# Softmax sums moved from GpSimd to VectorE, reciprocals to ScalarE as logarithm and exponential, with more buffers and a new order of steps

## Chip, cores and metric

The kernel runs on one core of one Trainium2 chip. The metric is the device time of one execution in microseconds (us). The kernel before takes 196.88 us, the median of 3 runs (196.62 to 197.10).

## What is computed

A layernorm `xn` of 2048 tokens of 512 features feeds two branches, which are summed with the input:

```python
# A: linear attention with a softmax feature map, 32 heads of 16
pq = einsum("bhsd,hdf->bhsf", q, w_phi); pk = einsum("bhsd,hdf->bhsf", k, w_phi)
phi_q = concat([softmax(pq), softmax(-pq)], -1)      # 16 + 16 features a head
phi_k = concat([softmax(pk), softmax(-pk)], -1)
kv = einsum("bhsf,bhsd->bhfd", phi_k, v);  z = phi_k.sum(over s)
o = (phi_q @ kv) / (phi_q @ z + 1e-6)                # then @ wo
# B: h = xn @ w1 + b1; act = h * tanh(softplus(h)); act @ w2, with 1792 hidden features
out = x + A(xn) + B(xn)
```

## The kernel before

Tokens are in 16 tiles of 128 and in four groups of four tiles. A short head loads the inputs, folds `w_phi` into the key weights and normalises the first group. All the rest is the list `STEPS`, a table of step names that one loop at the end of the kernel executes in the order in which it is written. Each step records its instructions; every engine executes its own in that order, and waits on semaphores for the others. So the table sets the order on each engine, and a step that waits holds back all that stands behind it on its engine.

The letters, with a group, stage or tile number behind them:

- `LN g`, `AP g k`: layernorm statistics of a group and their use on two tiles (VectorE, a little on GpSimd), then a transposing DMA into `xnT`.
- `V t`, `L s i`: one projection of four matmuls to values, or to logits; `VC`, `LC` evacuate them, on ScalarE (`a`) or VectorE (`v`). Stages `s` 0 to 3 are the keys of the four groups, 4 to 7 the queries. `F`, `FC` fold the query weights, from a transposed load `WT`.
- `H u`, `M u`: one of 56 hidden blocks, four matmuls (TensorE), and its Mish (ScalarE).
- `E s 0`, `E s 1`: maximum and minimum of each 16 logits by a tree of four VectorE operations, then a subtraction, into the tile `e`. `X s k`: the exponential of half a stage (ScalarE, in place).
- `S s k`: the sums of each 16 exponentials. In 15 of 16 cases they run on GpSimd (`p`), as a tree of four additions in `sums`; `S 6 0` runs on VectorE, one reduction.
- `R s k`: keys only, the inverses of the sums: a VectorE reciprocal, then a copy that doubles it, on VectorE (`v`) or GpSimd (`p`). `N s k`: the exponentials times the inverses (VectorE). `A g k`: 16 small matmuls a tile that accumulate keys times values. `KV`: the accumulated block masked into `kvm`.
- `W s k`: queries; the ratio of two sums, then one half of the features times it (VectorE), and two transposing DMAs into `qT`. `Q h i`: eight small matmuls against `kvm`; `G h i`: two ScalarE copies, numerators to `nm` and denominators to `ds`. `C h` (`combine`): reciprocal, doubled copy, product (VectorE), and a transposing DMA into `oT`.
- `O t`, `P t`, `Y t`: second layer (14 matmuls), output projection (4) and the residual with the store.

PSUM has six rotating banks for the projections, hidden blocks and outputs (tag `mm`) and one two-bank slot for `pkv`, `pnd` and `pwide`. The transposing DMAs and nearly all stores go through SP's queue.

Of the kernel before, what the change touches and what calls it, by code (L numbers as in the profile page):

```python
# [20 lines left out]


STEPS = """
LN 1; V 0; V 2; H 0; VC 2 a; H 1; M 0; M 1; H 2; H 3; H 4; M 2; H 5; H 6; M 3; M 4; M 5; E 0 0; E 0
1; M 6; H 7; H 8; M 7; H 9; H 10; M 8; M 9; AP 1 0; H 11; H 12; H 13; M 10; M 11; M 12; M 13; AP 1
1; LN 2; LN 3; V 1; L 1 0; VC 0 v; WL 1; X 0 0; V 3; L 1 3; VC 1 a; H 14; AP 2 0; AP 2 1; X 0 1; AP
3 0; S 0 0 p; LC 1 0 v; LC 1 3 a; V 5; VC 3 a; LC 1 1 v; H 15; M 14; AP 3 1; WL 2; M 15; VC 5 a; LC
1 2 v; E 1 0; H 16; H 17; V 4; M 16; M 17; H 18; M 18; H 19; M 19; H 20; H 21; M 20; M 21; VC 4 v; S
0 1 p; H 22; H 23; M 22; M 23; E 1 1; R 0 0 p; V 7; VC 7 v; X 1 0; V 6; L 2 0; LD; L 2 3; WT; R 0 1
v; L 2 2; S 1 0 p; LC 2 0 v; LC 2 3 a; L 2 1; LC 2 2 a; X 1 1; F 0; FC 0 a; S 1 1 p; H 24; M 24; VC  # L30
6 v; H 25; N 0 0; H 26; H 27; N 0 1; A 0 0; H 28; A 0 1; H 29; M 25; M 26; M 27; H 30; M 28; LC 2 1
v; E 2 0; F 1; H 31; M 29; V 11; R 1 0 p; M 30; E 2 1; M 31; H 32; M 32; L 3 0; F 2; X 2 1; S 2 1 p;
LC 3 0 a; L 3 2; L 3 1; FC 1 v; LC 3 2 v; V 8; X 2 0; S 2 0 p; VC 8 a; VC 11 v; LC 3 1 v; N 1 0; L 3
3; H 33; H 34; H 35; M 33; M 34; R 1 1 v; A 1 0; FC 2 v; H 36; LC 3 3 v; V 13; N 1 1; M 35; H 37; M
36; F 3; A 1 1; E 3 0; H 38; FC 3 a; H 39; H 40; M 37; M 38; L 4 1; L 4 0; M 39; E 3 1; V 9; VC 13
a; VC 9 v; M 40; LC 4 0 v; X 3 0; S 3 0 p; V 15; VC 15 v; V 12; L 4 2; LC 4 2 a; L 4 3; LC 4 3 a; H
41; X 3 1; V 10; R 2 1 v; VC 10 a; H 42; H 43; R 2 0 v; N 2 0; M 41; VC 12 a; S 3 1 p; A 2 0; N 2 1;
M 42; H 44; M 43; A 2 1; LC 4 1 v; H 45; M 44; E 4 0; E 4 1; M 45; R 3 0 p; H 46; H 47; H 48; M 46;
O 0; M 47; M 48; X 4 0; S 4 0 p; L 5 0; LC 5 0 a; R 3 1 v; N 3 0; L 6 2; N 3 1; V 14; L 5 2; L 5 1;
VC 14 a; LC 5 2 a; LC 5 1 a; X 4 1; L 5 3; LC 5 3 v; L 6 1; A 3 0; A 3 1; E 5 0; S 4 1 p; H 49; H  # L40
50; M 49; M 50; H 51; M 51; H 52; H 53; H 54; M 52; W 4 0; E 5 1; M 53; M 54; L 6 0; O 1; KV; X 5 0;
Q 0 0; G 0 0; L 6 3; LC 6 0 a; LC 6 1 v; H 55; W 4 1; LC 6 2 v; Q 0 1; G 0 1; C 0; O 2; O 3; LC 6 3
a; Q 1 0; M 55; O 4; X 5 1; G 1 0; E 6 0; S 5 0 p; W 5 0; E 6 1; Q 1 1; G 1 1; L 7 0; P 0; C 1; LC 7
0 a; P 1; X 6 0; O 5; Y 0; Y 1; S 5 1 p; Q 2 0; G 2 0; L 7 1; L 7 2; Q 2 1; W 5 1; P 2; P 3; LC 7 2
a; G 2 1; LC 7 1 a; S 6 0 v; W 6 0; L 7 3; C 2; Y 2; Q 3 0; O 6; LC 7 3 a; G 3 0; Q 3 1; O 7; O 8; P
4; Y 3; E 7 0; X 6 1; E 7 1; G 3 1; Q 4 0; O 9; P 5; Y 4; O 10; X 7 0; X 7 1; G 4 0; Q 4 1; G 4 1; C
3; P 6; P 7; S 6 1 p; W 6 1; Q 5 0; S 7 0 p; Y 5; W 7 0; O 11; G 5 0; Y 6; Y 7; Q 5 1; O 12; G 5 1;
Q 6 0; O 13; C 4; C 5; G 6 0; Q 6 1; P 8; P 9; S 7 1 p; G 6 1; W 7 1; Q 7 0; P 10; Y 8; Y 9; Y 10; C
6; P 11; G 7 0; Q 7 1; G 7 1; O 14; O 15; P 12; P 13; C 7; P 14; Y 11; Y 12; Y 13; Y 14; P 15; Y 15
"""  # L50


# [1 line left out]
def kernel(  # L54
# [164 lines left out]

    def mish(u):
        g, f = divmod(u, FT)
        nc.scalar.activation(  # L224
            acts[:, f, g * 512 : (g + 1) * 512], ph_of.pop(u)[:], ACT.Mish, bias=b1f[:, f : f + 1]
        )
# [6 lines left out]

    def take(s, i, copy):
        if i == 0:
            p_of[s] = smx.tile([P, TPG, 512], BF16, name="p_sb", bufs=1)
        copy(p_of[s][:, i, :], pl_of.pop((s, i)))  # L237

    def extremes(s, pl):

# [4 lines left out]
        src = pv
# [40 lines left out]
    def sums(s, k, pooled=False):

        t = smx.tile([P, 128], FP32, name="s")
        s_of[s, k] = t
        src = pair(s, k).rearrange("p t j l (c e) -> p (t j l c) e", e=16)  # L290
        if not pooled:
            nc.vector.reduce_sum(t[:], src, axis=AX.X)
            return
        for half in (8, 4, 2, 1):
            h = smx.tile([P, 128, half], FP32, name=f"h{half}", bufs=1)[:] if half > 1 else t[:, :, None]
            nc.gpsimd.tensor_tensor(  # L296
                out=h, in0=src[:, :, 0:half], in1=src[:, :, half : 2 * half], op=ALU.add
            )
            src = h

    r_of = {}

    def invert(s, k, pooled):

        t = s_of.pop((s, k))
# [8 lines left out]
    def normalise(s, k):

# [3 lines left out]
            op=ALU.mult,  # L319
        )  # L320

    def weigh(s, k):
# [4 lines left out]
        nc.vector.reciprocal(r[:], t[:, :, 1, :])
        nc.vector.tensor_tensor(  # L328
            out=r2[:], in0=t[:, :, 0, :, None].to_broadcast([P, 16, 4, 2]),
            in1=r[:, :, :, None].to_broadcast([P, 16, 4, 2]), op=ALU.mult,  # L330
        )
# [76 lines left out]
    def combine(h, parts=(slice(0, 2),)):

        nm, ds = nd_of.pop(h) if parts[-1].stop == 2 else nd_of[h]  # L410
        if h not in oT_of:
            oT_of[h] = lnp.tile([P, 8, P], BF16, name="oT")
        for q in parts:
            n = q.stop - q.start
            w = opool.tile([P, 2, 32], FP32, name="w")
            f = opool.tile([P, 2, 32, 2], BF16, name="f")
            nc.vector.reciprocal(w[:, q], ds[:, q].rearrange("p i j c -> p i (j c)"))
# [4 lines left out]
            v = nm[:, q].rearrange("p i j (c e o) -> p (i j c) e o", e=8, o=2)
            nc.vector.tensor_tensor(
                out=v, in0=v,
                in1=f[:, q].rearrange("p i c o -> p (i c) o")[:, :, None, :].to_broadcast(
                    [P, n * 32, 8, 2]
                ),
                op=ALU.mult,
            )
            nc.sync.dma_start_transpose(  # L430
                out=oT_of[h][:, 4 * q.start : 4 * q.stop, :],
                in_=nm[:, q].rearrange("p i j c -> p (i j c)"),
            )
# [164 lines left out]
```

## Time and profile before

| | |
|---|---|
| median of 3 runs | 196.88 us |
| the profiled execution's own time, and its span | 196.23 us, 194.5 us |
| mean granted TensorE clock | 0.982 |
| 40 to 50 us: busy PE, DVE, ACT, POOL | 8.14, 9.79, 8.39, 3.57 of 10 |
| 80 to 90 us | 6.35, 9.72, 7.70, 4.29 |
| 110 to 120 us | 7.08, 9.65, 4.24, 6.06 |
| 130 to 140 us | 7.38, 9.66, 3.59, 5.07 |
| 150 to 160 us | 9.95, 9.67, 2.38, 5.06 |
| 170 to 180 us | 9.89, 5.69, 2.24, 0.17 |
| granted clock, 50 to 60 and 120 to 130 us | 0.83, 0.85 |

PE is TensorE, DVE VectorE, ACT ScalarE, POOL GpSimd. A stretch's busy time counts an engine's own instructions; what it lacks to 10 us is waiting. The granted clock is the share of TensorE's full speed (2.4 GHz) that the chip gave.

### The profile page before, as it was taken

What the parts mean: (1) busy time and instruction counts of PE and PEld (TensorE: products, weight loads), DVE (VectorE), ACT (ScalarE), POOL (GpSimd) and SP (SyncE); (2) the same over time, 40 slices, a digit from 0 to 9 for tenths busy, and PEclk for the clock granted to TensorE, in tenths of its full rate; (3) what the DMA queues carried; (4) which work ended last, traced back from release to release, by engine and by line L of the source; (5) the groups of instructions that cost most, each with busy time, mean ns of one, the idle gap of its engine ahead of it and who ended that gap; (6) DMA issues with size and microseconds to landing.
All of it is one profiled execution on the core that took longest, in us unless ns stands there. A gap on an engine that the chain in (4) does not pass through costs nothing.

```text
span 194.5 us, 2775 instructions
## 1 busy us (share of the span) xinstructions
PE 173.2 (89%) x1023; PEld 83.9 (43%) x1039; DVE 167.5 (86%) x247; ACT 113.2 (58%) x153; POOL 88.1 (45%) x85
## 2 busy tenths in 40 slices
...
GB/s 149 310 401 172 109 17 191 310 277 19 0 0 0 0 3 0 0 0 0 5 0 0 0 3 108 110 54 19 102 175 164 82 27 57 135 192 185 110 110 108
DMA packets 44361, 18.02 MB, mean 93 GB/s; under 512 B 36796, under 2 KB 43836, under 8 KB 44348
## 3 DMA queue, kind: packets, MB, share of 16 engines
...
## 4 chain that ended last, share of the span: by engine, by line
DVE 56%; PE 31%; ACT 6%; issue 4%; DMA 2%; POOL 0%; DVEq 0%; POOLq 0%; ACTq 0%
DVE m L248 18%; DVE e L257 10%; PE ph L214 8%; PE po L442 8%; PE pproj L192 6%; DVE m L254 4%; PE po L450 3%; DVE e L335 3%; ACT e L272 3%; PE warm L496 3%; DVE q L328 3%; DVE p_sb L237 2%; DVE r L309 2%; DVE x_sb L458 2%; DVE e L317 2%
## 5 line engine op out<-in xcount | busy, mean ns | idle before, releaser
L214 PE MATMUL ph<-xnT,w_sb 128*128 128x512 bf16 x224 | 53.6, 390 | 3.2 <-DVE p_sb L237 2.3
L296 POOL TENSOR_TENSOR h<-e 128x1024 f32<-128x1024 bf16 x15 | 33.4, 2226 | 45.5 <-ACT e L272 31.5
L442 PE MATMUL po<-w_sb,acts 128*128 128x512 bf16 (+1 forms) x233 | 50.1, 366 | 2.8 <-ACT p_sb L237 2.6
L224 ACT ACTIVATE acts<-ph,b1f 128x512 bf16<-128x512 f32 x56 | 37.0, 691 | 8.7 <-PE ph L214 8.5
L296 POOL TENSOR_TENSOR h<-h 128x512 f32<-128x512 f32 (+1 forms) x30 | 34.4, 1147 | 2.4
L272 ACT ACTIVATE e<-e 128x2048 bf16<-128x2048 bf16 x16 | 30.5, 1914 | 8.4 <-DVE e L257 8.3
L214 PEld LDWEIGHTS <-w_sb 128*128 128x128 bf16 x224 | 22.0, 100 | 30.0 <-issue 7.0
L442 PEld LDWEIGHTS <-acts 128*128 128x128 bf16 x238 | 22.7, 98 | 25.9 <-issue 2.8
L192 PEld LDWEIGHTS <-xnT 128*128 128x128 bf16 x192 | 18.6, 99 | 25.9 <-issue 4.7
L248 DVE TENSOR_TENSOR m<-m 128x512 bf16<-128x512 bf16 (+1 forms) x32 | 22.0, 689 | 1.1
L192 PE MATMUL pproj<-wqk,xnT 128*128 128x512 bf16 x62 | 16.4, 395 | 3.1 <-ACT p_sb L237 1.9
L272 ACT ACT_TABLE_LOAD x7 | 9.0, 1283 | 16.5 <-DVE e L257 16.4
L458 DVE TENSOR_TENSOR x_sb<-po,x_sb 128x512 bf16<-128x512 f32 (+1 forms) x17 | 10.7, 653 | 8.5 <-PE po L450 8.5
L248 DVE TENSOR_TENSOR m<-p_sb 128x1024 bf16<-128x1024 bf16 x16 | 16.2, 1012 | 0.4
L192 PE MATMUL pproj<-wv,xnT 128*128 128x512 bf16 x59 | 15.5, 379 | 0.3
L237 ACT CAST p_sb<-pproj 128x512 bf16<-128x512 f32 x19 | 10.8, 587 | 8.1 <-PE pproj L192 4.3
L450 PE MATMUL po<-wqk,oT 128*128 128x512 bf16 (+1 forms) x65 | 14.7, 366 | 0.2
L401 ACT COPY ds<-pnd 128x32 f32<-128x32 f32 x16 | 2.9, 184 | 18.8 <-PE pnd L387 18.8
L192 PE MATMUL pproj<-wkp,xnT 128*128 128x512 bf16 x55 | 13.2, 379 | 0.2 <-DVE xnT L179 0.2
L257 DVE TENSOR_TENSOR e<-p_sb,m 128x2048 bf16<-128x2048 bf16 x8 | 12.4, 1544 | 0.6
L317 DVE TENSOR_TENSOR e<-e,r 128x2048 bf16<-128x2048 bf16 x8 | 11.3, 1438 | 0.1
L296 POOL TENSOR_TENSOR s<-h 128x128 f32<-128x128 f32 x15 | 10.8, 717 | 1.2
...
## 6 DMA issues: line engine op xcount, KB each, us to landing
...
```

Of the source, the lines that this page charges most:

```text
L192: nc.tensor.matmul(pp, lhsT=xnT[:, t, kt, :], rhs=w[:, kt, :], start=(kt == 0), stop=(kt == KT - 1),)
L214: nc.tensor.matmul(ph_of[u][:], lhsT=w1_sb[:, kt, f * P : (f + 1) * P], rhs=xnT[:, g * TPG : (g + 1) * TPG, kt, :], start=(kt == 0), stop= ...
L224: nc.scalar.activation(acts[:, f, g * 512 : (g + 1) * 512], ph_of.pop(u)[:], ACT.Mish, bias=b1f[:, f : f + 1])
L237: copy(p_of[s][:, i, :], pl_of.pop((s, i)))
L248: nc.vector.tensor_tensor(out=m[:], in0=src[:, :, 0:half], in1=src[:, :, half : 2 * half], op=op)
L257: nc.vector.tensor_tensor(out=e_of[s][:].rearrange("p t j l c -> p (t j) l c")[:, :, pl, :].rearrange("p t (c e o) -> p t c e o", e=8, o=2 ...
L272: nc.scalar.activation(v, v, ACT.Exp)
L296: nc.gpsimd.tensor_tensor(out=h, in0=src[:, :, 0:half], in1=src[:, :, half : 2 * half], op=ALU.add)
L317: nc.vector.tensor_tensor(out=vv, in0=vv, in1=r_of.pop((s, k))[:, :, None, :].to_broadcast([P, 128, 8, 2]), op=ALU.mult,)
L442: nc.tensor.matmul(po[:, c], lhsT=acts[:, f, t * P : (t + 1) * P], rhs=w2_sb[:, f, c], start=(f == 0), stop=False,)
L450: nc.tensor.matmul(po[:, c], lhsT=oT_of[t // 2][:, t % 2 * 4 + j, :], rhs=wo_sb[:, j, c], start=False, stop=(j == 3),)
L458: nc.vector.tensor_tensor(out=y, in0=po[:, c], in1=y, op=ALU.add)
```

## The change

`STEPS` is rewritten, and five functions change. Every `S` runs on VectorE. All eight `R` and all eight `C` take their inverse on ScalarE as exp(-log(s)), and one of eight `W` (`W 5 1`) its ratio as exp(log a - log b). One table set holds logarithm and exponential, and is asked for ahead of the step. The logits tile `p_sb` has two buffers for one, `e` three for two, `ds` four for two; the numerators `nm` and the transposed `oT` now lie in memory of weights and of `xnT` that is no longer read. Evacuations by VectorE: 7 of logits for 13, 5 of values for 7, 1 of folded weights for 2; the others go to ScalarE. Of the table, two rows, from the middle:

```diff
-E 0 0; ... S 0 0 p; ... R 0 0 p; ... W 4 0; E 5 1; M 53; M 54; L 6 0; O 1; KV; X 5 0; Q 0 0; G 0 0
+E 0 0; ... S 0 0; ... R 0 0 a; ... W 4 0 v; S 4 1; L 7 3; LC 7 3 a; L 7 2; LC 7 2 a; H 52; KV; Q 0 0; G 0 0
```

```diff
+    tables = [None]
+    def table(name):
+        if tables[0] != name:
+            tables[0] = name
+            if name != "mish_and_others":
+                nc.scalar.preload_act_table_set(name)
...
-            p_of[s] = smx.tile([P, TPG, 512], BF16, name="p_sb", bufs=1)
+            p_of[s] = smx.tile([P, TPG, 512], BF16, name="p_sb")
...
-            e_of[s] = epool.tile([P, TPG, 8, 2, 64], BF16, name="e")
+            e_of[s] = epool.tile([P, TPG, 8, 2, 64], BF16, name="e", bufs=3)
...
+    def sums(s, k):
+        t = s_of[s, k] = smx.tile([P, 128], FP32, name="s")
+        nc.vector.reduce_sum(
+            t[:], pair(s, k).rearrange("p t j l (c e) -> p (t j l c) e", e=16), axis=AX.X
+        )
+    def power(out, src, n, scale):
+        table("natural_log_exp_and_others")
+        nc.scalar.activation(
+            out, src.rearrange("p (c o) -> p c o", o=1).to_broadcast([P, n, 2]), ACT.Exp, scale=scale
+        )
+    def log(src, n):
+        table("natural_log_exp_and_others")
+        t = smx.tile([P, 128], FP32, name="log")
+        nc.scalar.activation(t[:, 0:n], src, ACT.Ln)
+        return t[:, 0:n]
+    def invert(s, k, how):
+        t = s_of.pop((s, k))
+        r2 = r_of[s, k] = smx.tile([P, 128, 2], BF16, name="r2")
+        if how == "a":
+            power(r2[:], log(t[:], 128), 128, -1.0)
             return
...
+        if how == "a":
+            t4 = log(t[:], 128).rearrange("p (t l c) -> p t l c", l=2, c=4)
+            nc.vector.tensor_tensor(
+                out=q[:], in0=t4[:, :, 0, :], in1=t4[:, :, 1, :], op=ALU.subtract
+            )
+            power(r2[:].rearrange("p t c o -> p (t c) o"), q[:].rearrange("p t c -> p (t c)"), 64, 1.0)
...
+            half = (wkp, wv)[h // 2 % 2][:, 2 * (h % 2) : 2 * (h % 2) + 2, :]
...
+    def combine(h, how):
+        nm, ds = nd_of.pop(h)
+        oT_of[h] = xnT[:, 2 * h : 2 * h + 2, :, :].rearrange("p t k c -> p (t k) c")
+        f = opool.tile([P, 64, 2], BF16, name="f")
+        d = ds[:].rearrange("p i j c -> p (i j c)")
+        if how == "a":
+            power(f[:], log(d, 64), 64, -1.0)
```

The first place is VectorE at the keys of groups 2 and 3 (`s` sums, `r2` doubled inverses, `e` exponentials). Before:

```order
L309 RECIPROCAL r_990<-s_766 128x128
L310 COPY r2_991<-r_990 128x256
L309 RECIPROCAL r_1005<-s_794 128x128
L310 COPY r2_1006<-r_1005 128x256
L317 TENSOR_TENSOR e_708<-e_708,r2_1006 128x2048
```

Now, at the keys of groups 1 and 2:

```order
L301 TENSOR_REDUCE s_790<-e_547 128x128
L336 TENSOR_TENSOR e_484<-e_484,r2_758 128x2048
L301 TENSOR_REDUCE s_877<-e_484 128x128
L301 TENSOR_REDUCE s_884<-e_547 128x128
L336 TENSOR_TENSOR e_484<-e_484,r2_879 128x2048
```

The reciprocals and copies have left VectorE, and reductions stand where they were; the products read inverses that come from ScalarE.

The second place is ScalarE behind the exponentials of the same keys (`log` logarithms; L284 and L272 are `X`). Before:

```order
L272 ACT_TABLE_LOAD
L272 ACTIVATE e_889<-e_889 128x2048
L237 CAST p_sb_945<-pproj_967 128x512
L237 CAST p_sb_945<-pproj_973 128x512
L272 ACTIVATE e_889<-e_889 128x2048
```

Now:

```order
L131 ACT_TABLE_LOAD
L318 ACTIVATE log_881<-s_877 128x128
L310 ACTIVATE r2_879<-log_881 128x256
L214 CAST vext0_102<-pproj_866 128x8x64
L248 CAST p_sb_690<-pproj_892 128x512
L318 ACTIVATE log_906<-s_790 128x128
L310 ACTIVATE r2_905<-log_906 128x256
L284 ACTIVATE e_770<-e_770 128x2048
```

Pairs of small activations stand between the evacuations and the exponentials. Over the kernel there are 13 table loads for 15.

The third place is VectorE around `kvm` (`KV`), for which the first `Q` waits. Before:

```order
L335 TENSOR_TENSOR e_1067<-e_1067,q2_1266 128x16x64
L248 TENSOR_TENSOR m8_1273<-p_sb_1138 128x1024
L248 TENSOR_TENSOR m4_1275<-m8_1273 128x512
L248 TENSOR_TENSOR m2_1277<-m4_1275 128x256
L254 TENSOR_TENSOR m1_1279<-m2_1277 128x256
L257 TENSOR_TENSOR e_1213<-m1_1279,p_sb_1138 128x32x64
L367 TENSOR_TENSOR kvm_88<-pkv_655,KVmask_101 128x8x64
```

Now:

```order
L336 TENSOR_TENSOR e_770<-e_770,r2_1147 128x2048
L354 RECIPROCAL q_1248<-s_1151 128x64
L355 TENSOR_TENSOR q2_1249<-s_1151,q_1248 128x128
L362 TENSOR_TENSOR e_1007<-e_1007,q2_1249 128x16x64
L301 TENSOR_REDUCE s_1256<-e_1007 128x128
L394 TENSOR_TENSOR kvm_88<-pkv_702,KVmask_101 128x8x64
```

A minimum tree (`E 5 1`) stood ahead of `kvm`; now a reduction (`S 4 1`) stands there, and both trees of stage 5 come earlier.

## Rows read from the trace of the kernel before

**Rows 1.** The page, busy time and share of the span by engine.

```profile
PE 173.2 (89%) x1023; PEld 83.9 (43%) x1039; DVE 167.5 (86%) x247; ACT 113.2 (58%) x153; POOL 88.1 (45%) x85
```

**Rows 2.** The page, the chain that ended last, by engine.

```profile
DVE 56%; PE 31%; ACT 6%; issue 4%; DMA 2%; POOL 0%; DVEq 0%; POOLq 0%; ACTq 0%
```

**Rows 3.** Waits of TensorE: total us, times, longest.

```profile
PE pnd L387 <- DVE kvm L373: 3.1, 1, 3.1
...
PE pkv L356 <- DVE e L317: 2.3, 1, 2.3
...
PE warm L496 <- POOL ident masks.py:199: 1.4, 1, 1.4
```

**Rows 4.** The chain of waits in order of time: start, us, what.

```profile
14.83 12.26 PE ph L214 x56
...
120.21 0.61 PE pnd L387 x8
...
164.32 3.23 DMA qT<-e
...
190.53 1.02 DVE x_sb L458 x2
```

**Rows 5.** VectorE's groups of instructions: xcount | busy us, mean ns | idle before.

```profile
L248 DVE TENSOR_TENSOR m<-p_sb 128x1024 bf16<-128x1024 bf16 x16 | 16.2, 1012 | 0.4
L248 DVE TENSOR_TENSOR m<-m 128x512 bf16<-128x512 bf16 (+1 forms) x32 | 22.0, 689 | 1.1
L254 DVE TENSOR_TENSOR m<-m 128x256 bf16<-128x256 bf16 x16 | 7.5, 472 | 0.5
L257 DVE TENSOR_TENSOR e<-p_sb,m 128x2048 bf16<-128x2048 bf16 x8 | 12.4, 1544 | 0.6
```

**Rows 6.** VectorE's timeline, 148.5 to 158.2 us: start, us, what.

```profile
148.64 0.68 DVE L248 TENSOR_TENSOR m<-p_sb 128x1024 bf16<-128x1024 bf16 x1
149.36 2.71 DVE L248 TENSOR_TENSOR m<-m 128x512 bf16<-128x512 bf16 x2
152.10 1.32 DVE L254 TENSOR_TENSOR m<-m 128x256 bf16<-128x256 bf16 x1
...
155.88 0.75 DVE L248 TENSOR_TENSOR m<-m 128x512 bf16<-128x512 bf16 x2
156.66 0.29 DVE L254 TENSOR_TENSOR m<-m 128x256 bf16<-128x256 bf16 x1
156.99 1.23 DVE L257 TENSOR_TENSOR e<-m,p_sb 128x2048 bf16<-128x2048 bf16 x1
```

**Rows 7.** GpSimd's timeline, same stretch.

```profile
149.79 2.12 POOL L296 TENSOR_TENSOR h<-e 128x1024 f32<-128x1024 bf16 x1 [14.03 <-DVE m L248]
```

**Rows 8.** One line each of VectorE: shortest, median and longest ns, over the span.

```profile
L335 DVE TENSOR_TENSOR e<-e,q x8: 691/875/1718, 115.1 to 174.3; 128x1024 bf16<-128x1024 bf16 x8
L328 DVE TENSOR_TENSOR q<-s,q x8: 291/538/2047, 114.2 to 173.9; 128x128 bf16<-128x128 f32 x8
```

**Rows 9.** VectorE's groups that leave, move or are added.

```profile
L309 DVE RECIPROCAL r<-s 128x128 bf16<-128x128 f32 x8 | 7.4, 938 | 0.0
L310 DVE COPY r<-r 128x256 bf16<-128x256 bf16 x5 | 5.6, 1114 | 0.2
L417 DVE RECIPROCAL w<-ds 128x64 f32<-128x64 f32 x8 | 4.4, 544 | 1.4 <-ACT ds L401 1.4
L237 DVE CAST p_sb<-pproj 128x512 bf16<-128x512 f32 x11 | 7.5, 682 | 0.6 <-PE pproj L192 0.6
L292 DVE TENSOR_REDUCE s<-e 128x128 f32<-128x2048 bf16 x1 | 2.3, 2277 | 0.0
```

**Rows 10.** ScalarE's groups of instructions.

```profile
L272 ACT ACTIVATE e<-e 128x2048 bf16<-128x2048 bf16 x16 | 30.5, 1914 | 8.4 <-DVE e L257 8.3
L404 ACT CAST nm<-pnd 128x512 bf16<-128x512 f32 x16 | 9.5, 592 | 1.6 <-DMA oT<-nm 1.6
L272 ACT ACT_TABLE_LOAD x7 | 9.0, 1283 | 16.5 <-DVE e L257 16.4
```

More of the change, by code (lines that the diff above doesn't have):

```diff
@@ L29 @@
[L29 to L48, printed above, removed]
@@ L49 @@
-6; P 11; G 7 0; Q 7 1; G 7 1; O 14; O 15; P 12; P 13; C 7; P 14; Y 11; Y 12; Y 13; Y 14; P 15; Y 15
+LN 1; V 3; VC 3 a; V 1; H 0; M 0; H 1; H 2; VC 1 a; H 3; H 4; M 1; M 2; H 5; M 3; M 4; M 5; H 6; H
+7; H 8; H 9; E 0 0; AP 1 0; AP 1 1; H 10; M 6; M 7; H 11; M 8; H 12; H 13; M 9; LN 2; E 0 1; M 10; M
+11; AP 2 0; H 14; L 1 3; WL 1; WL 2; AP 2 1; M 12; M 13; LN 3; X 0 0; L 1 0; X 0 1; H 15; L 2 1; L 2
+0; LC 1 0 a; LC 1 3 a; LC 1 2 a; LC 1 1 v; LC 2 0 a; L 2 2; S 0 0; AP 3 0; AP 3 1; L 2 3; LC 2 2 a;
@@ new lines @@
+WT; R 0 0 a; LC 2 1 v; E 1 0; H 16; LC 2 3 a; H 17; H 18; M 14; H 19; H 20; M 15; M 16; M 17; H 21;
+H 22; M 18; M 19; M 20; M 21; E 1 1; E 2 0; M 22; H 23; M 23; S 0 1; H 24; H 25; M 24; M 25; F 0; FC
+0 a; H 26; F 1; F 2; FC 2 v; H 27; H 28; FC 1 a; M 26; N 0 0; L 3 0; V 6; M 27; VC 6 v; M 28; F 3; X
+1 0; V 5; E 2 1; FC 3 a; V 0; VC 0 a; V 10; V 2; VC 2 v; LC 3 0 a; R 0 1 a; L 3 1; L 4 0; S 1 0; V
+9; VC 5 a; N 0 1; LC 4 0 a; L 4 2; V 7; A 0 0; X 2 0; X 1 1; VC 7 v; L 3 2; X 2 1; LC 4 2 v; L 3 3;
@@ new lines @@
+VC 9 v; V 4; A 0 1; VC 10 a; VC 4 a; R 1 0 a; H 29; LC 3 2 v; LC 3 3 v; LC 3 1 v; E 3 0; E 3 1; M
+29; S 2 0; N 1 0; LD; H 30; H 31; H 32; M 30; H 33; H 34; H 35; M 31; M 32; H 36; M 33; H 37; M 34;
+M 35; M 36; M 37; H 38; M 38; H 39; M 39; H 40; H 41; M 40; V 11; M 41; V 15; S 1 1; R 1 1 a; S 2 1;
+VC 11 a; V 13; L 4 1; LC 4 1 a; N 1 1; V 8; VC 8 v; R 2 0 a; N 2 0; L 5 3; L 4 3; A 1 0; X 3 1; VC
+13 a; R 2 1 a; LC 4 3 a; V 14; V 12; S 3 1; A 1 1; L 5 0; VC 12 a; A 2 0; LC 5 0 a; VC 15 a; R 3 1
@@ new lines @@
+a; H 42; LC 5 3 v; N 2 1; E 4 0; X 3 0; H 43; H 44; L 5 2; L 5 1; LC 5 2 a; VC 14 a; LC 5 1 a; M 42;
+E 4 1; M 43; L 6 0; S 3 0; A 2 1; E 5 0; E 5 1; N 3 1; M 44; L 7 0; LC 6 0 a; H 45; H 46; H 47; H
+48; M 45; M 46; H 49; H 50; M 47; M 48; M 49; M 50; H 51; M 51; X 4 0; R 3 0 a; S 4 0; O 0; X 4 1; O
+1; O 2; LC 7 0 a; X 5 0; N 3 0; A 3 0; X 5 1; L 6 1; LC 6 1 a; A 3 1; L 6 2; LC 6 2 a; W 4 0 v; S 4
+1; L 7 3; LC 7 3 a; L 7 2; LC 7 2 a; H 52; KV; Q 0 0; G 0 0; W 4 1 v; L 7 1; L 6 3; Q 0 1; LC 7 1 a;
@@ new lines @@
+LC 6 3 a; S 5 0; G 0 1; W 5 0 v; C 0 a; M 52; O 3; Q 1 0; G 1 0; H 53; H 54; M 53; E 6 0; M 54; Q 1
+1; G 1 1; S 5 1; O 4; Q 2 0; C 1 a; W 5 1 a; P 0; Y 0; E 6 1; E 7 0; O 5; G 2 0; Q 2 1; P 1; P 2; G
+2 1; Q 3 0; X 6 0; Y 1; C 2 a; S 6 0; P 3; O 6; Y 2; X 6 1; W 6 0 v; Y 3; O 7; G 3 0; Q 3 1; G 3 1;
+C 3 a; H 55; P 4; P 5; M 55; E 7 1; O 8; S 6 1; Q 4 0; W 6 1 v; Y 4; O 9; Y 5; X 7 0; S 7 0; W 7 0
+v; G 4 0; Q 4 1; P 6; P 7; O 10; G 4 1; C 4 a; Y 6; Q 5 0; G 5 0; O 11; Q 5 1; X 7 1; Y 7; O 12; G 5
@@ L50 @@
+1; S 7 1; C 5 a; Q 6 0; G 6 0; O 13; Q 6 1; W 7 1 v; P 8; P 9; G 6 1; C 6 a; Q 7 0; P 10; G 7 0; P
+11; Y 8; Y 9; Q 7 1; Y 10; O 14; G 7 1; O 15; C 7 a; P 12; P 13; Y 11; Y 12; Y 13; P 14; P 15; Y 14;
+Y 15
 """
@@ L204, in keep @@
         copy(
-            vext[(t // TPG) % 2][:, t % TPG, :, 0:64],
+            vext[t // TPG % 2][:, t % TPG, :, 0:64],
             pv_of.pop(t).rearrange("p (j c) -> p j c", j=8),
@@ L223, in mish @@
         g, f = divmod(u, FT)
+        table("mish_and_others")
         nc.scalar.activation(
@@ L284 @@
     s_of = {}
[L286 to L292, printed above, removed]
-            return
[L294 to L305, printed above, removed]
+    def sums(s, k):
[3 more added lines that the diff above has]
+        )
+    r_of = {}
+    def power(out, src, n, scale):
[4 more added lines that the diff above has]
+    def log(src, n):
+        table("natural_log_exp_and_others")
+        t = smx.tile([P, 128], FP32, name="log")
[6 more added lines that the diff above has]
+            power(r2[:], log(t[:], 128), 128, -1.0)
+            return
         r = smx.tile([P, 128], BF16, name="r")
-        r_of[s, k] = smx.tile([P, 128, 2], BF16, name="r2")
         with nc.allow_low_precision("the softmaxes are bf16"):
             nc.vector.reciprocal(r[:], t[:])
-        (nc.gpsimd if pooled else nc.vector).tensor_copy(
-            r_of[s, k][:], r[:].rearrange("p (c o) -> p c o", o=1).to_broadcast([P, 128, 2])
-        )
+        nc.vector.tensor_copy(r2[:], r[:].rearrange("p (c o) -> p c o", o=1).to_broadcast([P, 128, 2]))
     def normalise(s, k):
@@ L320, in normalise, with weigh @@
         )
-    def weigh(s, k):
-        t = s_of.pop((s, k))[:].rearrange("p (t l c) -> p t l c", l=2, c=4)
-        r = smx.tile([P, 16, 4], FP32, name="q")
+    def weigh(s, k, how):
+        t = s_of.pop((s, k))
+        q = smx.tile([P, 16, 4], FP32, name="q")
         r2 = smx.tile([P, 16, 4, 2], BF16, name="q2")
[L327 to L331, printed above, removed]
+        if how == "a":
[4 more added lines that the diff above has]
+            power(r2[:].rearrange("p t c o -> p (t c) o"), q[:].rearrange("p t c -> p (t c)"), 64, 1.0)
+        else:
+            t4 = t[:].rearrange("p (t l c) -> p t l c", l=2, c=4)
+            nc.vector.reciprocal(q[:], t4[:, :, 1, :])
+            nc.vector.tensor_tensor(
+                out=r2[:], in0=t4[:, :, 0, :, None].to_broadcast([P, 16, 4, 2]),
+                in1=q[:, :, :, None].to_broadcast([P, 16, 4, 2]), op=ALU.mult,
+            )
         vv = pair(s, k).rearrange("p t j l c -> p (t j) l c")[:, :, 1, :].rearrange(
```

44 lines of the change are left out of this document (11 added, 33 removed).

## The prediction

> **What bounds the kernel now.** I read the page first. TensorE is busy 173.2 us of the 194.5 us span, VectorE 167.5, ScalarE 113.2, GpSimd 88.1 [rows 1]. An average does not say which of the first two paces the other, so I read the chain of waits next: 56% of what ended last is VectorE and 31% TensorE [rows 2]. The waits of TensorE then show whom it waits for: `kvm` and `e` from VectorE, evacuated logits, and 1.4 us at the start for the identity [rows 3]. Its idle time can be counted: the last matmul ends at 190.5, 4.0 us before the span does [rows 4], so that 194.5 - 4.0 - 1.4 - 173.2 = 15.9 us are idle between its first and last matmul. The stretches in the table above put nearly all of it between 40 and 170 us, where VectorE is busy 9.6 to 9.8 us of 10 in the stretches that lack most. So VectorE sets the pace there, and TensorE is short of nothing but that.
>
> **Why VectorE is so long.** Part of its time is no work. One tree of four operations at 148.64 takes 0.68, 2.71 (two operations) and 1.32 us; the next tree, of the same shapes, has 0.75 for the two and 0.29 [rows 6]. The long ones lie where GpSimd runs its additions, from 149.79 on [rows 7]. The same spread is in the products of the queries: 291 ns at the shortest, 2047 at the longest, for one shape [rows 8].
>
> **The change, part by part.** I cost against the profiled execution, 196.23 us, that is 1.7 us beyond its span; the median of the three runs is 0.65 us higher.
>
> *GpSimd's additions go.* What VectorE loses with them is its stretched time, if GpSimd is the cause. From the groups, less the undisturbed durations: 16.2 - 16 x 0.68 = 5.3 for the first step of the trees, 22.0 - 16 x 0.75 = 10.0 for the two next, 7.5 - 16 x 0.29 = 2.9, and 12.4 - 8 x 1.23 = 2.6 for the subtraction [rows 5, 6]. The two operations of `W` give, by their medians, 8 x 0.18 + 8 x 0.25 = 3.5 [rows 8]. Sum: 24.3 us less.
>
> *VectorE gets the sums.* 15 reductions by 2.28 us [rows 9]: 34.2 us more. `S 6 0`, the one on VectorE already, is the row.
>
> *VectorE loses reciprocals and evacuations.* 7.4 for the keys' reciprocals, 5.6 for five doubled copies, 4.4 for the heads' reciprocals, and nine evacuations by 0.68, 6.1 [rows 9]: 23.5 us less. Together 167.5 - 24.3 + 34.2 - 23.5 = 154 us. That is 13 less than before, and 19 less than TensorE's 173.2.
>
> *ScalarE gets them.* No row shows a logarithm, or a broadcast input. The nearest are the exponential of 2048 elements, 1.91 us, and a copy of 512, 0.59 us [rows 10]. The line through them is 0.15 us and 0.86 ns an element: 0.26 for 128, 0.37 for 256, so 0.63 us for a key's inverse and 0.47 for a head's. I take these; the ends are 0.3 (fixed parts alone) and 1.2 (two copies of 512). Eight of each and the one ratio make 9.3 us, nine evacuations 5.3, and two table loads fewer save 2.6 [rows 10]: 113.2 + 12.0 = 125 us. ScalarE is idle for 81 us of the span before, so this costs nothing as work; as latency it lies between `S` and `N`, and costs where `N` stands right behind. In the new order `N` is mostly several VectorE operations behind its `S`.
>
> A table load here takes 1.28 us [rows 10]. The Trainium skill (ScalarE: Activation LUTs, Rules for kernel authors) budgets some 2.7 us for a switch of sets, and 0.3 us and 0.83 ns an element for an activation. By that a key's inverse would be 0.9 us and the two saved loads 5.4 us, an estimate from the page; ScalarE's sum would come to about 127 us, and neither figure would make it the bound.
>
> *Buffers and addresses.* A second `p_sb` lets evacuations of the next stage start while the trees of the last one run, and a third `e` lets a stage begin before `A` has read the one two back. `nm` and `oT` take memory whose readers (`V`, `L 3`, the hidden blocks of those tiles) stand before them in the table, so I price their new dependences at nothing; were one late, its price is a `Q` or `P` that waits, about the 3.2 us of a transposing DMA [rows 4].
>
> *The order.* `kvm` now stands behind a reduction and not behind the tree `E 5 1`. Up to `Q 0 0` TensorE has, by the new table, 95 steps of four matmuls and three of 14, 422 matmuls by 12.26 / 56 = 0.219 us [rows 4], that is 92.4 us from 13.1 (14.83 less two value projections). 144 small ones come to that, 11 us at most by the first eight of `Q`, which take 0.61 [rows 4]. `Q 0 0` can thus start between 105.5 and 116.4, against 120.2 now. VectorE has ahead of it 12 trees by about 3.0 (0.68 + 0.75 + 0.29 + 1.23) [rows 6], ten sums, eight products by 1.23 and 13 evacuations, 78 us of work, and its statistics as before; from its first tree on at about 14 us that ends soon enough. On SP's queue the loads of `w2` and `wo` now come after the last `AP` and the second `WT`, in a stretch where the DMA engines were idle before, some 30 us ahead of `O 0`. `WT` itself comes from a queue with nothing large in it; `F 0` stands nearer behind it, and may wait 1 to 2 us.
>
> **The sum.** If TensorE never waited, the span would be 1.4 + 173.2 + 4.0 = 178.6 us. Some waits stay, because all three engines now stand close together until `Q 0 0`: the load for `F 0` (0 to 2 us), hidden blocks that wait for a bank while ScalarE does exponentials (about 1 us), and products and sums that reach `A`, `Q` and `P` with a margin of one or two VectorE operations. I keep a third of the 15.9 us, 5.5, between bounds of 2 and 12. Span 184.1, time 185.8 by the profiled execution, **186.5 us** by the median, 5% less than before. The bounds of the kept waits give 183 and 193.
>
> **Rivals.**
>
> *The waits move to ScalarE.* Each inverse stands in ScalarE's order behind evacuations that wait for TensorE, an exponential of 1.91 us or a table load. Were the margins eaten at each half stage of the keys and queries, TensorE would keep 12 of its 15.9 us: 178.6 + 12 + 2.4 = 193. For it speaks the pair of activations in the chain; against it the 69 us in which ScalarE has nothing to do even with the change. Kept in full it would be no change, 196.9.
>
> *VectorE's stretched operations stay long.* Suppose they are long for their shapes or for banks, and not for GpSimd. Then VectorE has 34.2 - 23.5 = 10.7 us more work, in the stretch where it sets the pace: 207.6 us, slower. It decides at 10.7 of the 24.3 us: if less goes, the kernel loses. For it speaks the reduction's own price, by far the longest VectorE operation here. Against it speak equal shapes at 0.29 and 1.32 us within 5 us [rows 6], the long one beside an addition on GpSimd [rows 7]. The Trainium skill (VectorE: DVE Perf Modes, Rules for kernel authors) has a rule to this effect: expect the slowest mode from a reduction on a hot path, and restructure it. The trace agrees with the mode, at 2.28 us. The Trainium skill (SBUF — State Buffer, Who interferes with whom) says that a two-input operation of VectorE contends with a GpSimd operation that reads SBUF, and that a reduction never does; the durations above agree, and it is on that side.
>
> *TensorE's clock.* In two stretches before (50 to 60, 120 to 130 us), each behind one in which it idled, TensorE had a granted clock of 0.83 and 0.85 (the table above), between its two levels of 1.2 and 2.4 GHz. Fewer such dips would take up to 3 us off the 173.2; as many leave it. This is within the range.
>
> **How the numbers follow.** The forecast, 183 to 190 us, has a chance of 0.64; the waits on ScalarE, 190 to 196, 0.23; no change 0.03; VectorE longer, above 197.3, 0.10. Less than 0.2% from no change is what a measurement of this kernel can't tell. The range of 8 in 10 reaches from 182.5, little above the 181 of a TensorE that never waits, to 193.
>
> **What would show it.** Right: no additions on GpSimd, the trees' first steps at about 0.68 us throughout, VectorE at 154 us or under, TensorE idle for 2 to 8 us between its ends, the first `pnd` before 116 us. ScalarE near 125 us, a key's pair of activations near 0.63. Wrong: trees still at over 1 us; VectorE above 165; or TensorE's waits at over 10 us, named after `N` products that follow ScalarE's L310. A time above 193 with short trees would mean that the margins were not there.

## The result, and the profile after

The change takes 178.2 us, the median of 4 runs (177.77 to 178.57), against 196.97 us: a ratio of 0.905, 95% interval 0.902 to 0.907. The gain of 18.8 us is nearly twice the 10.4 that were forecast, and the time is below the range. The profiled execution took 178.57 us with a span of 176.8, and its granted clock was 1.00.

The page, busy time by engine, and the chain that ended last, by engine:

```profile
PE 169.3 (96%) x1039; PEld 82.9 (47%) x1039; DVE 143.3 (81%) x223; ACT 124.0 (70%) x194; POOL 8.6 (5%) x22
...
PE 79%; DMA 7%; ACT 6%; SPq 3%; DVE 2%; issue 1%; DVEq 0%
```

Against [rows 1, 2], VectorE is 24 us shorter, ScalarE 11 us longer, and another engine sets the pace: TensorE is 79% of the chain and VectorE 2%. TensorE itself is busy for 3.9 us less, with the same matmuls. (The trace of before holds records of 1023 of the 1039; what that hides is worked out below.)

All waits of TensorE (total us, times, longest):

```profile
PE warm L517 <- POOL ident masks.py:199: 1.4, 1, 1.4
PE ph L224 <- ACT p_sb L248: 1.1, 1, 1.1
PE ph L224 <- DMA w_sb<-in_B_w_dram: 1.0, 1, 1.0
PE pnd L414 <- DMA qT<-e: 0.4, 1, 0.4
PE pb L538 <- DVE wkp L154: 0.2, 1, 0.2
PE pproj L202 <- DVE xnT L189: 0.2, 1, 0.2
```

The waits for `kvm` and for `e` of [rows 3] are gone; what is left comes before 40 us but for 0.4. The first `pnd` and the last pieces, from the chain in order of time:

```profile
111.56 0.26 PE pnd L414 x8
...
172.86 1.02 DVE x_sb L479 x2
```

`Q 0 0` starts 8.7 us earlier than in [rows 4]. By the prediction's count TensorE is idle for 176.8 - 4.0 - 1.4 - 169.3 = 2.1 us between its ends. The waits listed above add up to more, 2.9 us without the 1.4 at the start. The 4.0 is the reason: 190.5 in [rows 4], and 172.86 here, is where VectorE's last residual starts, and TensorE is at work for 0.8 us more. From the timelines, before and after:

```profile
187.95 3.41 PE L450 MATMUL po<-wqk,oT 128*128 128x512 bf16 x19
...
170.06 3.63 PE L471 MATMUL po<-wqk,xnT 128*128 128x512 bf16 x20
```

So its work ends at 191.4 and at 173.7, 3.1 us ahead of the span's end both times, and the idle time after is 176.8 - 3.1 - 1.4 - 169.3 = 3.0 us.

VectorE's groups that answer to [rows 5, 9] (xcount | busy us, mean ns | idle before):

```profile
L301 DVE TENSOR_REDUCE s<-e 128x128 f32<-128x2048 bf16 x16 | 36.5, 2279 | 2.5 <-ACT log L318 1.4 <-ACT e L284 1.1
L259 DVE TENSOR_TENSOR m<-m 128x512 bf16<-128x512 bf16 (+1 forms) x32 | 11.5, 359 | 1.1
L259 DVE TENSOR_TENSOR m<-p_sb 128x1024 bf16<-128x1024 bf16 x16 | 10.9, 683 | 0.0
L268 DVE TENSOR_TENSOR e<-p_sb,m 128x2048 bf16<-128x2048 bf16 x8 | 9.8, 1226 | 0.7 <-DVE m L265 0.3
L265 DVE TENSOR_TENSOR m<-m 128x256 bf16<-128x256 bf16 x16 | 4.7, 292 | 0.5
```

The first line is the price paid, 36.5 us of reductions. The others are the same operations as before. In the order of the lines they take 359, 683, 1226 and 292 ns in the mean, where they took 689, 1012, 1544 and 472.

ScalarE's new groups:

```profile
L310 ACT ACTIVATE r<-log 128x256 bf16<-128x256 f32 x8 | 3.3, 416 | 0.3
L318 ACT ACTIVATE log<-s 128x128 f32<-128x128 f32 x9 | 2.8, 312 | 1.8 <-DVE s L301 1.8
L310 ACT ACTIVATE f<-log 128x128 bf16<-128x128 f32 x8 | 2.5, 310 | 0.3
L318 ACT ACTIVATE log<-ds 128x64 f32<-128x64 f32 x8 | 2.1, 265 | 0.0
```

A key's inverse, a logarithm and an exponential, is 0.73 us and a head's 0.58, each 0.1 above the line through the nearest rows.

### The profile page after: what moved, and what is told of

The parts are those of the page before. It is cut to its first block, busy times and chain, and to the rows that moved or that the text cites. A ratio compares the mean times of both kernels' runs of the same rounds, so it can differ in the third digit from the quotient of the medians.

```text
span 176.8 us, 2709 instructions
## 1 busy us (share of the span) xinstructions
PE 169.3 (96%) x1039; PEld 82.9 (47%) x1039; DVE 143.3 (81%) x223; ACT 124.0 (70%) x194; POOL 8.6 (5%) x22
## 4 chain that ended last, share of the span: by engine, by line
PE 79%; DMA 7%; ACT 6%; SPq 3%; DVE 2%; issue 1%; DVEq 0%
PE po L463 27%; PE ph L224 25%; PE pproj L202 17%; PE po L471 6%; DMA w_sb<-in_B_w_dram 5%; PE pkv L383 2%; PE pnd L414 2%; ACT e L284 2%; DMA qT<-e 2%; SPq L136 2%; DVE s L301 1%; ACT p_sb L248 1%; ACT acts L235 1%; ACT L235 1%; ACT L131 1%
## 5 line engine op out<-in xcount | busy, mean ns | idle before, releaser
L224 PE MATMUL ph<-xnT,w_sb 128*128 128x512 bf16 x224 | 50.5, 379 | 2.2 <-ACT p_sb L248 1.1
L301 DVE TENSOR_REDUCE s<-e 128x128 f32<-128x2048 bf16 x16 | 36.5, 2279 | 2.5 <-ACT log L318 1.4
L284 ACT ACTIVATE e<-e 128x2048 bf16<-128x2048 bf16 x16 | 30.1, 1904 | 0.8 <-DVE e L268 0.8
L202 PEld LDWEIGHTS <-xnT 128*128 128x128 bf16 x192 | 18.1, 98 | 20.9 <-DVE xnT L189 0.5
L248 ACT CAST p_sb<-pproj 128x512 bf16<-128x512 f32 x24 | 14.0, 585 | 6.1 <-PE pproj L202 5.9
L471 PE MATMUL po<-wqk,xnT 128*128 128x512 bf16 (+1 forms) x68 | 15.1, 366 | 0.0
L259 DVE TENSOR_TENSOR m<-m 128x512 bf16<-128x512 bf16 (+1 forms) x32 | 11.5, 359 | 1.1
L162 DVE BATCH_NORM_STATS2 stats<-x_sb 128x6 f32<-128x512 bf16 x16 | 10.0, 680 | 1.8 <-DMA x_sb<-in_A_x_dram 1.8
L259 DVE TENSOR_TENSOR m<-p_sb 128x1024 bf16<-128x1024 bf16 x16 | 10.9, 683 | 0.0
L268 DVE TENSOR_TENSOR e<-p_sb,m 128x2048 bf16<-128x2048 bf16 x8 | 9.8, 1226 | 0.7 <-DVE m L265 0.3
L268 DVE TENSOR_TENSOR e<-m,p_sb 128x2048 bf16<-128x2048 bf16 x8 | 9.8, 1225 | 0.3
L471 PEld LDWEIGHTS <-xnT 128*128 128x128 bf16 x68 | 6.2, 98 | 5.8
```

Source lines behind the costliest of these rows:

```text
L162: nc.vector.bn_stats(stats[:, i, :], x_sb[:, t0 + i, :])
L202: nc.tensor.matmul(pp, lhsT=xnT[:, t, kt, :], rhs=w[:, kt, :], start=(kt == 0), stop=(kt == KT - 1),)
L224: nc.tensor.matmul(ph_of[u][:], lhsT=w1_sb[:, kt, f * P : (f + 1) * P], rhs=xnT[:, g * TPG : (g + 1) * TPG, kt, :], start=(kt == 0), stop= ...
L259: nc.vector.tensor_tensor(out=m[:], in0=src[:, :, 0:half], in1=src[:, :, half : 2 * half], op=op)
L268: nc.vector.tensor_tensor(out=e_of[s][:].rearrange("p t j l c -> p (t j) l c")[:, :, pl, :].rearrange("p t (c e o) -> p t c e o", e=8, o=2 ...
L301: nc.vector.reduce_sum(t[:], pair(s, k).rearrange("p t j l (c e) -> p (t j l c) e", e=16), axis=AX.X)
```

## Experiments

Two questions. Which part of the change brings the time: VectorE's work (my theory), GpSimd's hands off it, or the order? And is it GpSimd that stretched VectorE's operations? "TensorE idle" below is the sum of its waits, without the 1.4 us at the start.

### The functions in the old order

```diff
-the new STEPS
+the STEPS of before: "S" -> sums(s, k), "R" -> invert(s, k, "a"), "C" -> combine(h, "a"), "W 5 1" by "a"
```

> All functions of the change (sums on VectorE, inverses and divisions on ScalarE, more buffers) in the order of steps of before, engines of the evacuations as before. Theory (VectorE's work is what paced the kernel, and the functions take it away): VectorE about 147 us, TensorE idle for a few us more than the 2.1 of the change, 180 to 187 us. Rival (the new order is what brought it): over 190 us.

215.6 us, ratio 1.094 (1.089 to 1.099). VectorE was busy 150.0 us, 17.5 less than in the kernel before, and the kernel was 19 us slower. VectorE's busy time doesn't say why; the waits do. ScalarE and VectorE from 61 to 81 us (timelines: start, us, what, idle before):

```profile
61.56 1.28 ACT L234 ACT_TABLE_LOAD   x1
62.85 1.84 ACT L234 ACTIVATE acts<-ph,b1f 128x512 bf16<-128x512 f32 x3
64.71 1.28 ACT L130 ACT_TABLE_LOAD   x1
66.01 1.91 ACT L283 ACTIVATE e<-e 128x2048 bf16<-128x2048 bf16 x1
...
74.34 0.69 ACT L234 ACTIVATE acts<-ph,b1f 128x512 bf16<-128x512 f32 x1 [2.36 <-PE ph L223]
76.05 0.69 ACT L234 ACTIVATE acts<-ph,b1f 128x512 bf16<-128x512 f32 x1 [1.02 <-PE ph L223]
76.75 1.28 ACT L130 ACT_TABLE_LOAD   x1
78.04 0.31 ACT L317 ACTIVATE log<-s 128x128 f32<-128x128 f32 x1
```

```profile
67.95 2.29 DVE L300 TENSOR_REDUCE s<-e 128x128 f32<-128x2048 bf16 x1 [4.37 <-ACT e L283]
...
78.39 2.29 DVE L300 TENSOR_REDUCE s<-e 128x128 f32<-128x2048 bf16 x1 [6.95 <-ACT log L317]
```

The logarithm stands behind two Mish steps, which wait for hidden blocks; the next sum waits for the logarithm, because there are two buffers for sums. ScalarE loads tables 21 times for the change's 13. The theory missed. The rival's "over 190" was met, but it had the order as a gain that comes beside the functions. In this order the functions, taken together, are a loss: the order decides their sign.

### The same with four buffers for the sums, and with the inverses on VectorE

```diff
-        t = s_of[s, k] = smx.tile([P, 128], FP32, name="s")
+        t = s_of[s, k] = smx.tile([P, 128], FP32, name="s", bufs=4)
```

> The old order with all functions of the change, as in the run old_order, but four buffers for the sums for two. There VectorE waited 11.7 us for ScalarE's logarithms to read a sum before the next one could be written. Theory (the sums' two buffers tie VectorE to ScalarE): those 11.7 us go, 202 to 207 us. Rival (the inverses on ScalarE are late in this order anyhow, and the wait only moves to the products): 211 to 216 us.

206.2 us, ratio 1.046 (1.042 to 1.050), as the theory had it: that wait is 9 us of the 19. VectorE's longest waits are now these, all for ScalarE but for the residual's:

```profile
DVE s L300 <- ACT e L283: 14.6, 6, 4.4
DVE x_sb L478 <- PE po L470: 10.5, 7, 4.4
DVE wv L450 <- ACT f L309: 9.0, 2, 7.9
DVE e L335 <- ACT r L309: 4.6, 2, 2.9
```

Then, in that kernel:

```diff
-invert(s, k, "a"), weigh(5, 1, "a"), combine(h, "a")
+invert(s, k, "v"), weigh(s, k, "v"), combine(h, "v")
```

> The same with the inverses, the ratio and the divisions on VectorE: old order, sums on VectorE, four buffers for the sums, the other new buffers. Theory (in this order the way through ScalarE, with its table loads between hidden blocks, is what costs): as the run sums_alone, 196 to 200 us. Rival (something else of the functions, such as the memory that nm and oT now share, costs in this order): over 203 us.

195.5 us, ratio 0.993 (0.991 to 0.996), a little under the theory's range; the rival, a cost of the memory that `nm` and `oT` share, did not come. So in the old order the way through ScalarE costs 10.7 us, though it takes 165.7 - 150.1 = 15.6 us off VectorE.

### The sums alone

```diff
-        "S": lambda s, k, c: sums(s, k, c == "p"),
+        "S": lambda s, k, c: sums(s, k),            # and bufs=4 for the sums
```

> The kernel before with all sums as one reduction on VectorE and four buffers for the sums; nothing else changes. Theory: 24 to 32 us of stretched operations go, 34 us of reductions come, VectorE 170 to 176 us, and it still paces: 195 to 203 us. Rival (taking the additions off GpSimd is the gain): 178 to 186 us.

198.3 us, ratio 1.0065 (1.005 to 1.008), within the theory's range. VectorE's busy time is 164.7 us for 167.5, where the theory had 170 to 176: what GpSimd's additions had stretched pays for the reductions, with 3 us to spare. It brings no time by itself; the kernel is 1.3 us slower.

### The new order with one function or both taken back

The inverses back on VectorE:

```diff
-        "R": invert, "W": weigh, "C": combine
+        "R": invert(.., "v"), "W": weigh(.., "v"), "C": combine(.., "v")
```

> The change with the inverses, the one ratio and the heads' divisions back on VectorE (reciprocal and doubled copy). VectorE 143 + 8 x (0.94 + 0.29) + 8 x (0.54 + 0.23) = about 159 us. Theory: still under TensorE's 169, so 179 to 185 us. Rival (VectorE needs all of its 26 us of room, or the chain through ScalarE is the shorter one): over 187 us, or under 178.

187.6 us, ratio 0.953 (0.951 to 0.955): the rival's side, if barely. VectorE is busy 159.4 us, as worked out, 11.5 below TensorE's 170.9, and yet TensorE is idle for 9.2 us. Room on an engine as a sum is not room at each step.

The sums back on GpSimd, inverses on ScalarE:

```diff
-        nc.vector.reduce_sum(t[:], src, axis=AX.X)
+        for half in (8, 4, 2, 1): nc.gpsimd.tensor_tensor(out=h, ..., op=ALU.add)   # not S 0 0, S 0 1, S 6 0
```

> The change with 13 of 16 sums back on GpSimd as a tree of four additions (the first two of the keys stay on VectorE; the partial sums of two are kept in bf16 for want of space); inverses stay on ScalarE. Theory: VectorE loses 13 x 2.28 = 30 us and gets 20 to 28 us of stretched operations, so its sum stays near 140 us, and only the longer way through GpSimd costs: 179 to 187 us. Rival (GpSimd off VectorE's back is the whole gain): over 190 us.

186.8 us, ratio 0.951 (0.946 to 0.957), at the end of the theory's range. VectorE is busy 141.0 us, 2 less than in the change, but it waits for sums that GpSimd has not finished:

```profile
DVE q L367 <- POOL s L313: 9.9, 5, 4.0
```

Both taken back, so that order, buffers and evacuations are left:

```diff
-        nc.vector.reduce_sum(t[:], src, axis=AX.X)
+        the four additions on GpSimd, as above; "R", "W", "C" by "v"
```

> The change's order, buffers and evacuations, but 13 of 16 sums on GpSimd (as before, the first two of the keys stay on VectorE, and two of the partial sums are kept in bf16 for want of space) and all inverses on VectorE. Theory: VectorE 159 - 13 x 2.28 + 20 to 28 of stretched operations, 150 to 158 us, and additions of over 5 us between exponentials and inverses: 184 to 193 us. Rival (order and buffers are the gain): 178 to 182 us. Rival (the stretched operations are the whole loss): over 193 us.

193.5 us, ratio 0.984 (0.981 to 0.986): half a microsecond beyond the theory's range, though VectorE's 155.4 us lie within what was worked out. The new order, its buffers and its evacuations are together worth 3.5 us; no run takes these three apart. (In the old order, with sums on VectorE, the new buffers brought 198.3 - 195.5 = 2.8 us.)

The runs as a table (us). The kernel before, and the 198.3 beside it, lack the new buffers but for the four of the sums. "GpSimd" is 15 of 16 sums in the old order and 13 in the new, and the order comes with its evacuations:

| order | sums | inverses | time | VectorE busy | TensorE busy, clock |
|---|---|---|---|---|---|
| old | GpSimd | VectorE | 197.0 | 167.5 | 173.2, 0.982 |
| old | VectorE | VectorE | 198.3 (195.5 with the new buffers) | 164.7 (165.7) | 172.8, 0.982 (169.9, 0.998) |
| old | VectorE | ScalarE | 206.2 (215.6 with two buffers for sums) | 150.1 (150.0) | 174.3, 0.975 (177.7, 0.942) |
| new | GpSimd | VectorE | 193.5 | 155.4 | 171.0, 0.991 |
| new | GpSimd | ScalarE | 186.8 | 141.0 | 173.2, 0.982 |
| new | VectorE | VectorE | 187.6 | 159.4 | 170.9, 0.991 |
| new | VectorE | ScalarE | 178.2 | 143.3 | 169.3, 1.000 |

Sums on VectorE cost 1 us in the old order, and bring 6 to 9 in the new. Inverses on ScalarE cost 11 in the old and bring 7 to 9 in the new.

### Work on GpSimd that nobody needs, reading or only writing

```diff
+        for _ in range(5):          # behind each sum: reads weights
+            nc.gpsimd.tensor_tensor(out=acts[:, 13, 1536:2048], in0=w1[:, 0:512], in1=w1[:, 512:1024], op=ALU.add)
```

> The change plus work on GpSimd that nobody needs: behind each sum five additions of 512 elements that read loaded weights and write a part of the activations that is not in use until late. No instruction of VectorE waits for it. Theory (two-input operations of VectorE are stretched by GpSimd operations that read): trees, subtractions and products stretched as before, some 20 to 30 us more on VectorE in the stretch where it is busy 9.6 of 10, 190 to 205 us; reductions and evacuations unchanged. Rival (they were long for their shapes): 178 us and 0.68, 0.42, 0.29 us as now.

```diff
+        for _ in range(10):         # instead: writes the same place
+            nc.gpsimd.memset(acts[:, 13, 1536:2048], 0.0)
```

> The same, but ten memsets of 512 elements on GpSimd in place of five additions: GpSimd writes the same place and reads nothing. Theory (it is the reading that collides): VectorE's durations as in the change, 178 us. Rival (any GpSimd work stretches VectorE): as the run with additions, over 190 us.

VectorE's trees, reductions and evacuations, with the additions, 107.9 us of them (220.0 us, ratio 1.118, 1.114 to 1.122):

```profile
L259 DVE TENSOR_TENSOR m<-m 128x512 bf16<-128x512 bf16 (+1 forms) x32 | 23.1, 723 | 1.1
L259 DVE TENSOR_TENSOR m<-p_sb 128x1024 bf16<-128x1024 bf16 x16 | 17.4, 1090 | 0.0
L301 DVE TENSOR_REDUCE s<-e 128x128 f32<-128x2048 bf16 x16 | 36.4, 2276 | 0.4 <-ACT log L323 0.4
L248 DVE CAST p_sb<-pproj 128x512 bf16<-128x512 f32 x6 | 3.9, 675 | 0.0
```

With the memsets, 84.1 us of them (183.9 us, ratio 0.938, 0.932 to 0.943):

```profile
L259 DVE TENSOR_TENSOR m<-m 128x512 bf16<-128x512 bf16 (+1 forms) x32 | 11.5, 359 | 1.1
L259 DVE TENSOR_TENSOR m<-p_sb 128x1024 bf16<-128x1024 bf16 x16 | 10.9, 683 | 0.0
```

and the longest wait of TensorE in it:

```profile
PE po L465 <- POOL acts L305: 2.9, 1, 2.9
```

The additions make the trees of two SBUF inputs 1.6 to 2 times as long, and leave the reduction and the evacuation from PSUM alone. VectorE goes from 143.3 to 184.7 us, more than the 20 to 30 of the theory, and the time is beyond its 190 to 205. The memsets leave trees and reductions as they are in the change, to the nanosecond.

The memsets do touch one operation of VectorE, the layernorm's `xn`, which reads one tile and two numbers a partition. Its last four, between 37.8 and 40.2 us, run beside the memsets. From VectorE's timelines, the change and then the memsets:

```profile
37.80 1.38 DVE L174 TENSOR_SCALAR xn<-x_sb,mv,rstd 128x512 bf16<-128x512 bf16 x4
...
37.91 2.27 DVE L174 TENSOR_SCALAR xn<-x_sb,mv,rstd 128x512 bf16<-128x512 bf16 x4
```

That is 0.9 us in all. With the additions the same group of 16 takes 571 ns in the mean, for 461 with the memsets and 405 in the change.

The kernel with the memsets is 5.7 us slower than the change, where the theory had none, and that comes from where I put them: the last hidden block writes the same place. In the profiled execution TensorE waited 2.9 us for them at 161 us, and its granted clock from 160 to 180 us was 0.83. The Trainium skill (SBUF — State Buffer, Who interferes with whom) says that a two-input operation of VectorE contends with a GpSimd operation that reads SBUF and not with one that only writes it, and that a reduction never does. The trees and reductions of the two runs agree on each point.

### Less for TensorE

The last of 14 hidden blocks is left out of the second layer.

```diff
-            for f in range(FT):
+            for f in range(FT - 1):
```

> The change without the last of 14 hidden blocks in the second layer: 17 matmul groups shorter by one, 15 of 512 columns and two of 256, 16 x 0.216 = 3.5 us of TensorE's work left out, all else the same. Theory (TensorE now paces nearly everywhere): 174.8 us, all of it saved. Rival (VectorE is close behind): 176.5 to 178 us.

175.5 us, ratio 0.893 (0.891 to 0.895): between the theory's 174.8 and the rival's 176.5. By the medians 2.7 us came back, by the profiled executions 3.1. TensorE's busy time fell by 3.2, to 166.1, and not by the 3.5 worked out. The wait for the hidden layer's weights fell by 0.6 us, and this one, 0.4 us in the change, grew by as much:

```profile
PE pnd L414 <- DMA qT<-e: 1.0, 1, 1.0
```

TensorE sets the pace, and the transposed queries are less than a microsecond behind.

### Two of the waits that are left

Value projection 0 moved into the first of them:

```diff
-LN 1; V 3; VC 3 a; V 1; H 0; ... FC 3 a; V 0; VC 0 a; V 10;
+LN 1; V 3; VC 3 a; V 1; V 0; VC 0 a; H 0; ... FC 3 a; V 10;
```

> The change with one step moved: value projection 0 and its evacuation stand ahead of the first hidden block, where TensorE waits 0.98 us for the hidden layer's weights. Theory (TensorE paces): 0.86 us of its work goes into the wait, 177.3 us. Rival (the wait is made up elsewhere): 178.2 us.

178.3 us, ratio 0.906 (0.904 to 0.908): a miss, as the rival had it. TensorE waits no longer at 14.5 us, but 0.7 us for `vext` at 60 us, where `V 0` had stood. It also waits 0.7 us at 6.4 us, ahead of the moved step, which the change's trace doesn't show. Then, in that kernel, two evacuations of logits moved ahead, both now by VectorE:

```diff
-LC 1 0 a; LC 1 3 a; LC 1 2 a; LC 1 1 v; LC 2 0 a;
+LC 1 0 v; LC 1 1 v; LC 1 3 a; LC 1 2 a; LC 2 0 a;
```

> The same, and the first two logits of group 1 are evacuated by VectorE ahead of ScalarE's (one more evacuation on VectorE), so that the first reduction need not wait for ScalarE's evacuations, 7.0 us of waiting in the change, nor TensorE 1.07 us for a bank at 38 us. Theory: both waits go, 176.3 us. Rival (hidden blocks then wait for ScalarE's Mish instead): as the run before, 177.3 us.

176.0 us, ratio 0.895 (0.893 to 0.897), 2.2 us under the change and the fastest of the kernels that do the whole work. All waits of TensorE:

```profile
PE warm L491 <- POOL ident masks.py:199: 1.4, 1, 1.4
PE pb L512 <- DVE wkp L128: 0.3, 1, 0.3
PE pproj L176 <- DVE xnT L163: 0.2, 1, 0.2
```

The waits at 38 and at 60 us both went. In the timelines VectorE ends the first reduction at 35.6 us and not at 37.9.

## Why the prediction was right and wrong

**The bound, right.** VectorE set the pace, and stretched operations made it long. That GpSimd's additions, which read SBUF, stretched them is shown by the two runs with useless work. The rival in which the operations stay long did not come.

**VectorE's sum, 10 us too long.** I had 154 us, it is 143.3. The step "8 x 0.18 + 8 x 0.25 = 3.5" took medians, and most of the time lay in a few long ones. The two operations of `W`, before and then after:

```profile
L335 DVE TENSOR_TENSOR e<-e,q 128x1024 bf16<-128x1024 bf16 x8 | 8.9, 1112 | 0.4
L328 DVE TENSOR_TENSOR q<-s,q 128x128 bf16<-128x128 f32 x8 | 7.3, 918 | 0.3
...
L362 DVE TENSOR_TENSOR e<-e,q 128x1024 bf16<-128x1024 bf16 x8 | 5.5, 692 | 0.6 <-ACT q L310 0.4
L355 DVE TENSOR_TENSOR q<-s,q 128x128 bf16<-128x128 f32 x7 | 2.0, 292 | 0.2
```

They lost 8.7 us (0.2 of it came back, as the subtraction of two logarithms in `W 5 1`). I had also left out the stretched products of the keys (1.6 us less) and of the heads (0.8), and the heads' doubled copies (1.8).

**ScalarE's sum, right, in part by luck.** 124.0 us for 125. The new activations took 11.0 us for 9.3, an inverse 0.73 where the line gave 0.63, and the Mish steps and exponentials, which I had left as they were, took 1.5 less. The Trainium skill's figures (ScalarE: Activation LUTs, Rules for kernel authors) gave 0.9 for an inverse, an estimate; the rows lie between.

**The floor, the first step that failed, by 3.9 us.** "If TensorE never waited, the span would be 1.4 + 173.2 + 4.0 = 178.6 us" used busy time that held slow matmuls: it is 169.3 with the clock at 1.00 throughout. I had seen the two stretches at 0.83 and 0.85 and said "up to 3 us" and "This is within the range". Neither the sum nor the range's lower end, 182.5, has it in, though a TensorE that waits less is the very thing that was forecast. In the table busy time and clock go together: 169.3 at 1.000, 170.9 at 0.991, 173.2 at 0.982, 177.7 at 0.942, for the same matmuls, give or take the microsecond that missing records hide (below). Ahead of each of the two stretches TensorE had idled, 2.3 us at 48 and 3.1 us at 117. These two waits were paid twice, as idle time and as slow matmuls behind them. Not every wait was: behind those of 1.9 to 2.6 us at 88, 103 and 136 us the clock stayed at 1.00. No run shows what tells them apart.

**The waits that stay, the second, by 3.4 us.** "I keep a third of the 15.9 us, 5.5, between bounds of 2 and 12": by the same count it was 2.1. Of the waits that I named, two came, a bank at 38 us (1.07 us; I had about 1) and 0.4 us for transposed queries at 128 us. The 1.0 us for the hidden layer's weights I had not named, and the load for `F 0` held up nothing. The margins at the later joints, which I had thought would be eaten, held. I took a third for want of a reason.

The two make 184.1 - 176.8 = 7.3 us. The last 1.0 of 186.5 - 178.2 is that this profiled execution took 0.4 us more than its median, where that of before took 0.65 less.

**Two slips that cancel.** The 15.9 us are right by luck. The end at 190.5 is 0.9 us too early, so by busy time TensorE idled for 16.8 us; but 16 of its matmuls have no record, and the time of these looks idle. Its waits alone, listed and without the one at the start, come to 15.9. Counted by waits, 194.5 - 3.1 - 1.4 - 15.9 = 174.1 us were work, and after the change 176.8 - 3.1 - 1.4 - 2.9 = 169.4. So the floor was wrong by 4.7 us and the waits by 2.6, with the same sum. The two slow stretches lack 1.7 and 1.5 us of full clock (an estimate, ten microseconds each by what the clock lacks to 1.00); the rest of the 4.7 is open.

**The rival of ScalarE's waits** did not come in this order; in the old one it did, in full and beyond, and made the kernel slower than before. I had priced it as a share of TensorE's idle time. The runs show that the order decides it, by what stands ahead of a logarithm (Mish steps, table loads) and by how long a sum's buffer is held.

**The signs** that I gave for the mechanism came: no additions on GpSimd, the trees' first steps at 0.68 us, VectorE under 154, TensorE idle for 2 to 3 us, `pnd` at 111.6 us. Only a key's pair of activations is off, 0.73 for 0.63.
